# Issuing w_in earlier and putting pairs 6 to 12 and the weights on one software DMA queue, in a fused attention and MLP kernel

## The chip, the cores and the metric

The kernel runs on one core of one Trainium2 chip. The metric is the device time of one execution in microseconds (us). Executions of this kernel spread by one to two per cent. Two things in the traces differ from execution to execution: stretches of *half clock*, in which the trace's record of the clock granted to TensorE shows 0.5 instead of 1.0, and the rate of the DMA engines. So small differences are read from ratios with their 95% interval and from traces. "Ratio" below is always the mean time of one kernel's fast runs over that of the other kernel's fast runs of the same rounds, so it is not quite the ratio of the medians that are quoted. A difference under 2% is called "the same".

In the views PE is TensorE, PEld its weight loads, DVE VectorE, ACT ScalarE, POOL GpSimd and SP SyncE.

## The reference

```
q, k, v: float32 (8 batches, 12 heads, 448 rows, 64)
attn = softmax(q @ k.T / 8) @ v                        # per batch and head
x    = attn, heads side by side: (3584, 768)
h    = x @ w_in                                        # w_in (768, 2048) float32
out  = max(0.01 * h, h) @ w_out                        # w_out (2048, 768) float32; out (3584, 768)
```

## The kernel before

Work on attention is cut into 48 *pairs* (two heads of one batch; six pairs are a batch). For each pair, q, k and v come by DMA as float32 (three loads of 224 KB), GpSimd casts them to bf16, TensorE (for the first twelve pairs) transposes q and k, then computes scores and the product with v. When a batch is ready, the MLP over it is interleaved with the attention of the next batch. The first batch is done in twelve *halves* so that the first MLP can start after about 30 us.

Two kinds of DMA queue are in play. Loads of pairs are issued by SyncE on a hardware queue. The weights, which are cast on the way, are issued by GpSimd on a software queue; w_in in four column quarters, w_out in two row halves times two column halves. In each case at most eight transfers of an issuer are in flight: the trace shows eight semaphores for each, and a further issue waits until one has landed.

```python
    def load(u, queues=(nc.sync,) * 3):           # three DMAs: q, k, v of pair u
        ...                                       # buffers: five pairs in rotation
    def cast(u, by=(nc.gpsimd.tensor_copy,) * 3):
        ...

    for i in range(4):
        w_steps.append((w_in_sb[:, :, ts(i, DF // 4)], w_in_v[:, :, ts(i, DF // 4)]))
    for i in range(4):
        at = (slice(None), ts(i % 2, MD // 2), ts(i // 2, NW))
        w_steps.append((w_out_sb[at], w_out_v[at]))

    load(0, (nc.sync, nc.scalar, nc.sync))
    for i in range(1, 5):
        load(i)
    # ... memsets
    cast(0, (nc.vector.tensor_copy, nc.scalar.copy, nc.gpsimd.tensor_copy))
    cast(1)
    cast(2)
    # ... in the half stage, after half h:
    half_loads = {0: 5, 5: 6, 8: 7, 10: 8}
    half_casts = {1: 3, 3: 4, 5: 5, 8: 6, 10: 7}
    half_w = {5: 4, 8: 2, 10: 2}                  # how many weight pieces to issue
    half_turns = {1: 1, 2: 2, 4: 3, 5: 4, 7: 5, 11: 6}   # TensorE transposes of these pairs
    # ... later, pair by pair (u = 6, 7, ...):
    loads = {6: (9,), 7: (10, 11), 8: (12, 13)}   # then u + 5
    #   transposes(u + 1), cast(u + 3) (and cast(8) at u = 6)
    # second matmul of the first MLP: first column half of all chunks, then the second
        todo = [(c, w) for c in range(n // P) for w in range(2)]
        if i == 0:
            todo.sort(key=lambda cw: cw[1])
```

The softmax here doesn't subtract the row's maximum and nothing guards it: scores larger than these inputs give would overflow.

Of the kernel before, what the change touches and what calls it, by code (L numbers as in the profile page):

```python
# [9 lines left out]
F32 = mybir.dt.float32  # L10
# [6 lines left out]
def kernel(  # L17
# [9 lines left out]
    nc = tc.nc  # L27

    B, H, S, D = q.shape
    DM, DF = moe_w_in.shape  # L30
    P = 128
    HP = H // 2
# [3 lines left out]
    MD = DF // P  # L36
    NW = DM // 2
# [3 lines left out]
    cuts = [((b * S) // P) * P for b in range(B)] + [B * S]  # L41
# [15 lines left out]
    o_pool = ctx.enter_context(tc.tile_pool(name="o", bufs=3))  # L57
# [4 lines left out]
    ps_mm = ctx.enter_context(tc.tile_pool(name="ps_mm", bufs=2, space=PSUM))  # L62
# [23 lines left out]
    w_out_sb = w_pool.tile([P, MD, DM], BF16)  # L86
    w_in_v = moe_w_in.rearrange("(ko ki) n -> ki ko n", ki=P)
    w_out_v = moe_w_out.rearrange("(ko ki) n -> ki ko n", ki=P)
# [6 lines left out]
    def load(u, queues=(nc.sync,) * 3):  # L95
        if u >= NU:
            return
        b, hp = divmod(u, HP)
        raw[u] = []
        for a, name, eng in zip((q, k, v), ("fq", "fk", "fv"), queues):  # L100
            t = ld_pool.tile([SC, 2, NSC, D], F32, name=name)
            eng.dma_start(  # L102
                out=t.rearrange("p h so d -> p h (so d)"),
                in_=a[b, 2 * hp:2 * hp + 2].rearrange("h (p so) d -> p h (so d)", so=NSC),
            )
            raw[u].append(t)

    def cast(u, by=(nc.gpsimd.tensor_copy,) * 3):
        if u >= NU:
            return  # L110
        fq, fk, fv = raw.pop(u)
        qk_sb[u] = cast_pool.tile([SC, 2, NSC, 2, D], BF16, name="qkb")
        by[0](qk_sb[u][:, 0].rearrange("p so h d -> p h so d"), fq)  # L113
        by[1](qk_sb[u][:, 1].rearrange("p so h d -> p h so d"), fk)  # L114
        by[2](v_sb[u % NV][:, :, :, :D], fv)  # L115

    w_steps = []
    for i in range(4):
        w_steps.append((w_in_sb[:, :, ts(i, DF // 4)], w_in_v[:, :, ts(i, DF // 4)]))
    for i in range(4):  # L120
        at = (slice(None), ts(i % 2, MD // 2), ts(i // 2, NW))
        w_steps.append((w_out_sb[at], w_out_v[at]))

    def load_w(n=1):
        for _ in range(n):
            if w_steps:
                o, i = w_steps.pop(0)
                nc.gpsimd.dma_start(out=o, in_=i)  # L128
# [8 lines left out]
    def warm_up(n):  # L137
        for _ in range(n):
            ps = ps_mm.tile([P, 512], F32, name="mm")
            nc.tensor.matmul(ps, warm[:, :P], warm, start=True, stop=True)  # L140
# [10 lines left out]
        nc.gpsimd.memset(t[:, QL:], 0.0)  # L151
    cast(0, (nc.vector.tensor_copy, nc.scalar.copy, nc.gpsimd.tensor_copy))
    cast(1)
    cast(2)


    x_t = {}
# [76 lines left out]
    def half_scores(h, cp):  # L234
        u, ph = halves[h]
        ps = ps_s.tile([P, 2, 512], F32, name="sc")
        t = qkT[u % NQ]
        for i in range(2):
            c = 2 * cp + i
            for j in range(2):  # L240
                nc.tensor.matmul(  # L241
                    ps[:, j, ts(i, SH)],
                    t[j * D:(j + 1) * D, S + c * SC:S + c * SC + P],
                    t[j * D:(j + 1) * D, ts(ph, SH)],
                    start=True, stop=True,
                )
        e = e_sb[h % NE][:, :EH].rearrange("p (j c s) -> p j c s", j=2, c=NSC)
        nc.scalar.activation(  # L248
            e[:, :, 2 * cp:2 * cp + 2, :],
            ps[:SC, :, :S].rearrange("p j (c s) -> p j c s", c=2), AX.Exp, scale=scale,  # L250
        )
# [25 lines left out]
    def half_x_transposes(h):  # L277
        u, ph = halves[h]
        x = xh_t.pop(h)
        tr = ps_tr.tile([P, 2, S], BF16, name="tr")  # L280
        for qc in range(2):
            nc.tensor.transpose(tr[:, 0, ts(qc, SC)], x[:, qc], ident[:SC, :SC])
        nc.vector.tensor_copy(xT[:, u, ts(ph, SH)], tr[:, 0, :SH])
        if u == HP - 1:
            ready[0] = (ph + 1) * SH


    def store(o, t0):

        done = 0  # L290
        while done < P:
            b, j = divmod(t0 + done, S)
            so, p = divmod(j, SC)
            n = min(SC - p, P - done)
            dst = out[b * S:(b + 1) * S].rearrange("(p so) n -> so p n", so=NSC)
            nc.sync.dma_start(out=dst[so, p:p + n], in_=o[done:done + n, :])
            done += n

    def mlp(i):
        n = cuts[i + 1] - cuts[i]  # L300
        at = cuts[i] % NX
        h = h_pool.tile([P, MD, 4 * P], BF16, name="h")
        for lo, hi in ((0, SH), (SH, n)) if i == 0 else ((0, n),):
            for m in range(MD):
                ps = ps_mm.tile([P, 4 * P], F32, name="mm")
                assert i or hi <= ready[0]
                for kk in range(KD):
                    nc.tensor.matmul(  # L308
                        ps[:, :hi - lo], w_in_sb[:, kk, ts(m, P)], xT[:, kk, at + lo:at + hi],
                        start=(kk == 0), stop=(kk == KD - 1),  # L310
                    )
                    if kk == KD - 1:
                        nc.scalar.activation(  # L313
                            h[:, m, lo:hi], ps[:, :hi - lo], AX.Prelu, alpha=0.01
                        )
                    yield hi - lo

        todo = [(c, w) for c in range(n // P) for w in range(2)]
        if i == 0:
            todo.sort(key=lambda cw: cw[1])  # L320
        o = {}
        for c, w in todo:
            if c not in o:
                o[c] = o_pool.tile([P, DM], F32, name="o")
            ps = ps_mm.tile([P, 4 * P], F32, name="mm")
            for m in range(MD):
                nc.tensor.matmul(  # L327
                    ps[:, :NW], h[:, m, ts(c, P)], w_out_sb[:, m, ts(w, NW)],
                    start=(m == 0), stop=(m == MD - 1),
                )  # L330
                if m == MD - 1:
                    nc.vector.tensor_copy(o[c][:, ts(w, NW)], ps[:, :NW])  # L332
                    if w == 1:
                        store(o.pop(c), cuts[i] + c * P)
                yield NW


    loads = {6: (9,), 7: (10, 11), 8: (12, 13)}
    half_loads = {0: 5, 5: 6, 8: 7, 10: 8}
    half_casts = {1: 3, 3: 4, 5: 5, 8: 6, 10: 7}  # L340
    half_w = {5: 4, 8: 2, 10: 2}
    half_turns = {1: 1, 2: 2, 4: 3, 5: 4, 7: 5, 11: 6}

    def half_slots(h):


        def s0():
            half_scores(h, 0)

        def s1():  # L350
            if h == 0:
                warm_up(2)
            if h >= 2:
                half_x_transposes(h - 2)

        def s2():
            half_scores(h, 1)
            if h == 0:
                warm_up(2)

        def s3():
            if h in half_turns:
                transposes(half_turns[h])
            if h >= 1:
                half_pv(h - 1)
            if h in half_loads:
                load(half_loads[h])
            if h in half_casts:
                cast(half_casts[h])
            load_w(half_w.get(h, 0))  # L370

        return [s0, s1, s2, s3]

# [2 lines left out]
    def slots(u):  # L376

        on = u < NU

        def s0():  # L380
            if on:
                scores(u, 0)
                scores(u, 1)
                expo(u, 0)

        def s1():
            if on:
                expo(u, 1)
            if u - HP < 2:
                half_x_transposes(NH - 2 + u - HP)  # L390
            elif u <= NU + 1:
                x_transposes(u - 2)
            dma_transposes(u + 2)

        def s2():
            if u == HP:
                half_pv(NH - 1)
            elif u <= NU:
                pv(u - 1, 0)

        def s3():
            for i in loads.get(u, (u + 5,)):
                load(i)
            if u + 1 < NU:
                transposes(u + 1)

        def s4():
            if on:
                scores(u, 2)
                scores(u, 3)  # L410
                expo(u, 2)

        def s5():
            if on:
                expo(u, 3)
            if u == HP:
                cast(u + 2)
            cast(u + 3)

        def s6():  # L420
            if HP < u <= NU:
                pv(u - 1, 1)

        def s7():
            pass

        return [s0, s1, s2, s3, s4, s5, s6, s7]

    steps = [s for h in range(NH) for s in half_slots(h)]
# [9 lines left out]
    for i in range(B):  # L439
        work = steps[begin[i]:begin[i + 1]] if i + 1 < B else []  # L440
        n = cuts[i + 1] - cuts[i]
# [42 lines left out]
```

## Time and profile before

| | before |
|---|---|
| time, median of 3 (range) | 437.7 us (437.5 to 439.06) |
| profiled execution | 442.64 us, span 440.8 us |
| TensorE idle for w_in | 9.7 us in three waits |
| half clock in the trace's clock record | 32.8 to 39.6 us and 53.3 to 60.1 us |
| first w_in DMA: issued, first packet, landed | 22.2, 27.3, 35.6 us |
| last w_in quarter landed; last w_out piece landed | 54.3; 74.7 us |

From 60 us on TensorE is never short of work for long, so only the first 60 us can give time. The first view is of TensorE's waits over the whole kernel before: who waited, for whom, total us, number of times, longest.

```profile
PE mm L308 <- DMA w_in_sb<-in_moe_w_in_dram: 9.7, 3, 5.8
PE tr L282 <- DVE xh L269: 3.2, 9, 0.5
```

The timeline of TensorE before shows where: start, duration, the operation, and in brackets the idle time in front of it and what ended it.

```profile
35.63 1.12 PE L308 MATMUL mm<-xT,w_in_sb 128*128 128x224 bf16 x5 [5.77 <-DMA w_in_sb<-in_moe_w_in_dram]
...
48.04 2.03 PE L308 MATMUL mm<-xT,w_in_sb 128*128 128x224 bf16 x19 [0.89 <-DMA w_in_sb<-in_moe_w_in_dram]
...
54.32 1.11 PE L308 MATMUL mm<-xT,w_in_sb 128*128 128x224 bf16 x5 [3.08 <-DMA w_in_sb<-in_moe_w_in_dram]
```

GpSimd's timeline before has the four issues of w_in in one line, only after the cast of pair 5:

```profile
22.21 3.43 POOL L128 DMA_DIRECT2D w_in_sb<-in_moe_w_in_dram  x4
```

And the table by stretches before (from:to, length, busy us of PE, PEld, DVE, ACT and POOL with the number of instructions, granted TensorE clock, share of the DMA engines, GB/s written; the share can exceed 1, as the times of packets overlap):

```profile
30.00:35.00 5.00, 0.00 (x0) 0.00 (x0) 0.00 (x0) 0.88 (x1) 3.60 (x6) 0.78 1.18 246
35.00:40.00 5.00, 4.37 (x39) 3.27 (x40) 0.67 (x3) 1.27 (x3) 1.73 (x3) 0.54 1.18 245
...
50.00:55.00 5.00, 1.92 (x16) 1.28 (x16) 0.28 (x1) 2.33 (x4) 0.00 (x0) 0.83 1.19 248
55.00:60.00 5.00, 5.00 (x43) 3.52 (x42) 1.23 (x3) 1.45 (x3) 0.00 (x0) 0.50 1.22 248
```

A wait costs twice: the idle time itself, and the work behind it that runs at half clock (0.54 and 0.50). Meanwhile the DMA engines are full in every row. w_in is not late because the engines rest; it is late because other bytes went first: by 27 us the hardware queue alone had fetched more pairs than the six that the half stage needs.

### The profile page before, as it was taken

What the parts mean: (1) busy time and instruction counts of PE and PEld (TensorE: products, weight loads), DVE (VectorE), ACT (ScalarE), POOL (GpSimd) and SP (SyncE); (2) the same over time, 40 slices, a digit from 0 to 9 for tenths busy, and PEclk for the clock granted to TensorE, in tenths of its full rate; (3) what the DMA queues carried; (4) which work ended last, traced back from release to release, by engine and by line L of the source; (5) the groups of instructions that cost most, each with busy time, mean ns of one, the idle gap of its engine ahead of it and who ended that gap; (6) DMA issues with size and microseconds to landing.
All of it is one profiled execution on the core that took longest, in us unless ns stands there. A gap on an engine that the chain in (4) does not pass through costs nothing.

```text
span 440.8 us, 9314 instructions
## 1 busy us (share of the span) xinstructions
PE 419.2 (95%) x3875; PEld 235.6 (53%) x3875; DVE 102.0 (23%) x289; ACT 233.6 (53%) x338; POOL 92.2 (21%) x171
## 2 busy tenths in 40 slices
PE   8757699999999999999999999999999999999995
PEld 3535476654455555554455555554455555554563
DVE  2531122432122211232122211232122211220021
ACT  4763657656753377545753377545753477304300
POOL 4593112232211121313111131313111100000000
PEclk9997979999999999999999999999999999999999
DMA  9999999378655677587555687577555531130022
GB/s 200 237 241 245 246 231 201 42 218 211 132 110 139 171 186 173 138 167 186 117 107 143 165 200 168 133 162 192 115 107 144 152 87 26 48 81 13 0 73 71
DMA packets 98506, 63.67 MB, mean 144 GB/s; under 512 B 55456, under 2 KB 94880, under 8 KB 98464
## 3 DMA queue, kind: packets, MB, share of 16 engines
q1 hardware_dynamic: 90928, 56.56, 55.1%
q0 software_dynamic: 7296, 6.29, 8.8%
q8 instruction: 30, 0.49, 0.5%
q10 hardware_dynamic: 240, 0.23, 0.2%
q14 instruction: 12, 0.10, 0.1%
HBM read 45.61 MB, written 11.01 MB: 128 GB/s over the span
## 4 chain that ended last, share of the span: by engine, by line
PE 86%; DMA 11%; POOL 1%; issue 0%; ACT 0%; DVE 0%; SPq 0%; POOLq 0%
PE mm L327 34%; PE mm L308 33%; PE pv L204 10%; PE sc L186 9%; DMA w_in_sb<-in_moe_w_in_dram 7%; DMA fv<-in_v_dram 2%; DMA fq<-in_q_dram 2%; DMA fk<-in_k_dram 1%; PE tr L174 0%; POOL w_in_sb L128 0%; ACT e L195 0%; POOL v L115 0%; PE tr L225 0%; DVE o L332 0%; SPq L102 0%
## 5 line engine op out<-in xcount | busy, mean ns | idle before, releaser
L195 ACT ACTIVATE e<-sc 112x896 bf16<-112x896 f32 x168 | 148.1, 915 | 100.1 <-PE sc L186 99.6
L308 PE MATMUL mm<-xT,w_in_sb 128*128 128x512 bf16 (+3 forms) x864 | 167.4, 337 | 10.4 <-DMA w_in_sb<-in_moe_w_in_dram 9.7
L327 PE MATMUL mm<-w_out_sb,h 128*128 128x384 bf16 x896 | 161.2, 326 | 0.0
L308 PEld LDWEIGHTS <-w_in_sb 128*128 128x128 bf16 x864 | 76.5, 99 | 80.3 <-issue 18.1
L327 PEld LDWEIGHTS <-h 128*128 128x128 bf16 x896 | 81.3, 98 | 62.3 <-issue 14.8
L313 ACT ACTIVATE h<-mm 128x512 bf16<-128x512 f32 (+3 forms) x144 | 72.5, 504 | 71.5 <-PE mm L308 71.2
L115 POOL CAST v<-fv 112x512 bf16<-112x512 f32 x48 | 29.7, 618 | 236.3 <-PE pv L204 203.0
L211 DVE RECIPROCAL rec<-pv 112x4 f32<-112x4 f32 x84 | 15.3, 183 | 204.9 <-PE pv L204 204.7
L204 PEld LDWEIGHTS <-e 112*128 112x128 bf16 x1344 | 54.5, 98 | 12.2
L204 PE MATMUL pv<-v,e 112*128 112x65 bf16 x1344 | 57.2, 194 | 0.0
L332 DVE COPY o<-mm 128x384 f32<-128x384 f32 x56 | 31.2, 557 | 85.0 <-PE mm L327 84.7
L186 PE MATMUL sc<-qkT 64*128 64x448 bf16 x336 | 46.7, 357 | 0.0
L212 DVE TENSOR_TENSOR x<-pv,rec 112x256 bf16<-112x256 f32 x84 | 35.6, 424 | 2.9
L113 POOL CAST qkb<-fq 112x512 bf16<-112x512 f32 x47 | 29.0, 616 | 19.6 <-DMA fq<-in_q_dram 12.1
L114 POOL CAST qkb<-fk 112x512 bf16<-112x512 f32 x47 | 29.0, 616 | 4.5 <-DMA fk<-in_k_dram 4.0
L248 ACT ACTIVATE e<-sc 112x896 bf16<-112x896 f32 x24 | 21.5, 916 | 6.9 <-PE sc L241 6.6
L186 PEld LDWEIGHTS <-qkT 64*128 64x128 bf16 x336 | 9.6, 94 | 27.5 <-issue 23.6
L241 PE MATMUL sc<-qkT 64*128 64x224 bf16 x96 | 9.0, 266 | 1.6 <-DVE qkT L177 1.3
L177 DVE COPY qkT<-tr 128x896 bf16<-128x896 bf16 x12 | 7.5, 625 | 10.3 <-PE tr L174 10.2
L261 PE MATMUL pv<-v,e 112*128 112x65 bf16 x192 | 8.6, 198 | 0.0
L261 PEld LDWEIGHTS <-e 112*128 112x128 bf16 x192 | 7.6, 101 | 0.8 <-issue 0.6
L174 PE MATMUL tr<-ident,qkb 112*128 112x112 bf16 x96 | 7.4, 223 | 0.3
(28 smaller groups left out, 47.1 us busy)
## 6 DMA issues: line engine op xcount, KB each, us to landing
fq<-in_q_dram SPq DMA_DIRECT2D x48, 224.0 KB, 3.8
fv<-in_v_dram SPq DMA_DIRECT2D x48, 224.0 KB, 4.0
fk<-in_k_dram SPq DMA_DIRECT2D x47, 224.0 KB, 4.0
w_in_sb<-in_moe_w_in_dram POOLq DMA_DIRECT2D x4, 768.0 KB, 21.3
w_out_sb<-in_moe_w_out_dram POOLq DMA_DIRECT2D x4, 768.0 KB, 38.4
out_dram<-o SPq DMA_DIRECT2D x8, 336.0 KB, 3.0
out_dram<-o SPq DMA_DIRECT2D x8, 288.0 KB, 2.7
out_dram<-o SPq DMA_DIRECT2D x8, 240.0 KB, 3.1
```

Of the source, the lines that this page charges most:

```text
L113: by[0](qk_sb[u][:, 0].rearrange("p so h d -> p h so d"), fq)
L114: by[1](qk_sb[u][:, 1].rearrange("p so h d -> p h so d"), fk)
L115: by[2](v_sb[u % NV][:, :, :, :D], fv)
L186: nc.tensor.matmul(ps[:, j, :S], t[j * D:(j + 1) * D, S + c * SC:S + c * SC + P], t[j * D:(j + 1) * D, :S], start=True, stop=True,)
L195: nc.scalar.activation(e[:, :, c, :], sc_t.pop((u, c))[:SC, :, :S], AX.Exp, scale=scale)
L204: nc.tensor.matmul(ps[:, qc, :], e[:, at:at + P], vt[:, j, c, :], start=(c == 0), stop=(c == NSC - 1),)
L212: nc.vector.tensor_mul(x_t[u][:, :, j, :], ps[:SC, :, :D], rec.to_broadcast([SC, NSC, D]))
L248: nc.scalar.activation(e[:, :, 2 * cp:2 * cp + 2, :], ps[:SC, :, :S].rearrange("p j (c s) -> p j c s", c=2), AX.Exp, scale=scale,)
L308: nc.tensor.matmul(ps[:, :hi - lo], w_in_sb[:, kk, ts(m, P)], xT[:, kk, at + lo:at + hi], start=(kk == 0), stop=(kk == KD - 1),)
L313: nc.scalar.activation(h[:, m, lo:hi], ps[:, :hi - lo], AX.Prelu, alpha=0.01)
L327: nc.tensor.matmul(ps[:, :NW], h[:, m, ts(c, P)], w_out_sb[:, m, ts(w, NW)], start=(m == 0), stop=(m == MD - 1),)
L332: nc.vector.tensor_copy(o[c][:, ts(w, NW)], ps[:, :NW])
```

## The change

Intent: have w_in there when the first MLP starts, and give TensorE the rest in the order of use. Two quarters of w_in are issued between the casts of the first pairs. Pairs 6 to 12 leave the hardware queue and stand with the weights in the one software queue. w_out comes in four row quarters, and the second matmul of the first MLP takes its chunks in plain order. The casts of pairs 9 to 11 also move back by one pair in the program (`casts`).

```diff
-        at = (slice(None), ts(i % 2, MD // 2), ts(i // 2, NW))
-        w_steps.append((w_out_sb[at], w_out_v[at]))
+        w_steps.append((w_out_sb[:, ts(i, MD // 4), :], w_out_v[:, ts(i, MD // 4), :]))
     cast(1)
+    load_w()
     cast(2)
+    load_w()
-        if i == 0:
-            todo.sort(key=lambda cw: cw[1])
 ... (the loop over chunks c and column halves w in plain order)
-    loads = {6: (9,), 7: (10, 11), 8: (12, 13)}
-    half_loads = {0: 5, 5: 6, 8: 7, 10: 8}
-    half_w = {5: 4, 8: 2, 10: 2}
+    behind = {5: (6, "w", "w", 7), 8: ("w", "w", 8), 10: ("w", "w", 9)}
+    behind_pair = {6: (10,), 7: (11,), 8: (12,)}
+    casts = {6: (8,), 7: (9,), 8: (10,), 9: (11, 12)}
+    def issue(what):
+        for i in what:
+            if i == "w":
+                load_w()
+            else:
+                load(i, (nc.gpsimd,) * 3)
 ... (in slots:)
-            for i in loads.get(u, (u + 5,)):
-                load(i)
+            if u >= 8:
+                load(u + 5)
```

More of the change, by code (lines that the diff above doesn't have):

```diff
@@ L316, in mlp @@
                     yield hi - lo
-        todo = [(c, w) for c in range(n // P) for w in range(2)]
-        if i == 0:
-            todo.sort(key=lambda cw: cw[1])
-        o = {}
-        for c, w in todo:
-            if c not in o:
-                o[c] = o_pool.tile([P, DM], F32, name="o")
-            ps = ps_mm.tile([P, 4 * P], F32, name="mm")
-            for m in range(MD):
-                nc.tensor.matmul(
-                    ps[:, :NW], h[:, m, ts(c, P)], w_out_sb[:, m, ts(w, NW)],
-                    start=(m == 0), stop=(m == MD - 1),
-                )
-                if m == MD - 1:
-                    nc.vector.tensor_copy(o[c][:, ts(w, NW)], ps[:, :NW])
-                    if w == 1:
-                        store(o.pop(c), cuts[i] + c * P)
-                yield NW
-    loads = {6: (9,), 7: (10, 11), 8: (12, 13)}
-    half_loads = {0: 5, 5: 6, 8: 7, 10: 8}
-    half_casts = {1: 3, 3: 4, 5: 5, 8: 6, 10: 7}
-    half_w = {5: 4, 8: 2, 10: 2}
+        for c in range(n // P):
+            o = o_pool.tile([P, DM], F32, name="o")
+            for w in range(2):
+                ps = ps_mm.tile([P, 4 * P], F32, name="mm")
+                for m in range(MD):
+                    nc.tensor.matmul(
+                        ps[:, :NW], h[:, m, ts(c, P)], w_out_sb[:, m, ts(w, NW)],
+                        start=(m == 0), stop=(m == MD - 1),
+                    )
+                    if m == MD - 1:
+                        nc.vector.tensor_copy(o[:, ts(w, NW)], ps[:, :NW])
+                    yield NW
+            store(o, cuts[i] + c * P)
+    half_casts = {1: 3, 3: 4, 5: 5, 8: 6, 10: 7}
+    behind = {5: (6, "w", "w", 7), 8: ("w", "w", 8), 10: ("w", "w", 9)}
[7 more added lines that the diff above has]
+                load(i, (nc.gpsimd,) * 3)
     half_turns = {1: 1, 2: 2, 4: 3, 5: 4, 7: 5, 11: 6}
@@ L365, in s3 @@
                 half_pv(h - 1)
-            if h in half_loads:
-                load(half_loads[h])
+            if h == 0:
+                load(5)
             if h in half_casts:
                 cast(half_casts[h])
-            load_w(half_w.get(h, 0))
+            issue(behind.get(h, ()))
         return [s0, s1, s2, s3]
@@ L415, in s5 @@
                 expo(u, 3)
-            if u == HP:
-                cast(u + 2)
-            cast(u + 3)
+            for i in casts.get(u, (u + 3,)):
+                cast(i)
+            issue(behind_pair.get(u, ()))
         def s6():
```

## The prediction

> **What bounds the kernel now.** From 60 us on TensorE is busy in every window (the windows view shows 10.00 of 10 us to 400 us), so only the first 60 us can give time. There the waits view puts 9.7 us of TensorE idleness on the landing of w_in: 5.8 us before the first MLP matmul at 35.6, 0.9 before 48.0, 3.1 before 54.3. After the long gaps the granted clock is 0.54 (35 to 40 us) and 0.50 (55 to 60 us), where about 4 and 5 us of work run at half rate: another 4.5 us, an estimate. Sum: about 14 us. The Trainium skill (TensorE: Matmul & The Clock Gate, Part 1) tells of a free-running window of about 3.4 us after which an idle array is halved; the trace agrees.
>
> The reason is DMA order. Until 27 us the hardware queue alone runs, at 237 to 242 GB/s (0.97 us for each 224 KB load), and has fetched some ten pairs although the half stage needs six. The first w_in DMA is issued at 22.2 us, its first packet moves at 27.3; then both queues share and a quarter of w_in lands only every 6.3 us. The last w_in lands at 54.3, w_out not until 74.
>
> **What the change does.** Two quarters of w_in are issued at about 9.5 and 13 us. With the same 5 us of delay they flow from 14.6 us beside pairs 4 and 5 (84 packets per engine, 0.131 us per pair of packets of the two queues): pair 5 lands at about 25.6 instead of 21.5. I expect its transposes to wait 1 to 2 us, and the MLP to start near 31 to 32 us with two quarters present. The w_in waits go.
>
> But the rest is in one queue behind the cast of pair 5: about 27 us, then a bubble of about 2 us in the DMA engines. From there, sequentially: a pair 2.9 us (at the rate of a queue alone), a weight quarter 3.8 us (w_out alone read about 410 GB/s of f32 at 62 to 66 us). Pair 6 at 31.5, w_in complete at 39, pair 7 at 42, w_out's first half at 50, pair 8 at 53, w_out complete at 61, pair 9 at 63 to 65, later if pair 13 on the hardware queue mixes in. TensorE would want the transposes of pairs 7, 8 and 9 at about 39, 47 and 54: so the waits for w_in become waits for q and k of pairs 7, 8, 9 (2 to 4 us each, half clock behind some). Pair 9's transposes ran at 65.3 before; I expect 61 to 66. The software issues cost GpSimd 0.75 us each, 16 us in all, beside 21% busy: off the path. The row quarters of w_out make packets of 1536 instead of 768 bytes[...]: nearly nothing. The new order of the second matmul's chunks: nothing, as w_out lands before 74.
>
> **Prediction.** Of the 14 us most comes back as waits for pairs: 436.5 us, 430.5 to 442.5 eight times in ten. Faster by over 2%: 0.07, same: 0.86, slower: 0.07.
>
> **What would show it.** Right: no wait for w_in; TensorE first MLP matmul near 32 us; waits of transposes for casts of pairs 7 to 9, GpSimd waiting on landing q, k of those; a half clock between 40 and 65. Wrong: TensorE without a gap after 32 us (then some 10 us faster), or w_in waits that remain.
>
> **What would make it wrong.** The software queue alone moving 1 KB packets faster or slower than 0.07 us each; a start delay of 5 us at each software issue; GpSimd held at an issue (eight may be in flight) while a cast is due; gaps too short for the clock to fall.

## The result, and the profile after

| | before | changed |
|---|---|---|
| median (range), 4 runs each | 438.02 us (437.5 to 439.06) | 440.73 us (440.39 to 441.48) |
| ratio, 95% interval | | 1.0061 (1.0037 to 1.0085) |
| span of the profiled execution | 440.8 us | 438.6 us |
| TensorE idle for w_in | 9.7 us | 0 |
| TensorE idle for casts of pairs 7, 8, 9 | 0 | 8.1 us |
| half clock | 6.8 + 6.8 us | 3.4 + 3.4 us |

The timed runs say the same within 2%, a little slower. The two profiled executions seem to say the opposite (438.6 against 440.8), because the one of before fell in a slow execution with long stretches of half clock.

TensorE's waits after:

```profile
PE tr L175 <- POOL qkb L113: 6.8, 3, 3.2
PE tr L283 <- DVE xh L270: 3.2, 9, 0.5
...
PE tr L175 <- POOL qkb L114: 1.2, 3, 0.6
```

The waits for w_in have gone, and new ones of nearly the same sum have come: the transposes (tr) of q and k wait for GpSimd's casts (qkb). TensorE's timeline after has them one by one. The first line is the first MLP matmul, at 29.8 instead of 35.6 us and without a gap:

```profile
29.76 0.65 PE L309 MATMUL mm<-xT,w_in_sb 128*128 128x224 bf16 x5
...
41.37 0.37 PE L175 MATMUL tr<-ident,qkb 112*128 112x112 bf16 x4 [2.92 <-POOL qkb L113]
...
52.64 0.37 PE L175 MATMUL tr<-ident,qkb 112*128 112x112 bf16 x4 [3.20 <-POOL qkb L113]
53.57 0.56 PE L175 MATMUL tr<-ident,qkb 112*128 112x112 bf16 x4 [0.57 <-POOL qkb L114]
...
62.53 0.37 PE L175 MATMUL tr<-ident,qkb 112*128 112x112 bf16 x4 [0.71 <-POOL qkb L113]
63.39 0.37 PE L175 MATMUL tr<-ident,qkb 112*128 112x112 bf16 x4 [0.49 <-POOL qkb L114]
```

These are pairs 7, 8 and 9. GpSimd's timeline after shows what held the casts, here for pair 8: the cast of k waited for the DMA. (The line above it is an issue that waited for one of the eight transfers in flight.)

```profile
51.20 0.66 POOL L102 DMA_DIRECT2D fv<-in_v_dram  x1 [4.81 <-DMA w_out_sb<-in_moe_w_out_dram]
51.97 0.61 POOL L113 CAST qkb<-fq 112x512 bf16<-112x512 f32 x1
52.90 0.61 POOL L114 CAST qkb<-fk 112x512 bf16<-112x512 f32 x1 [0.32 <-DMA fk<-in_k_dram]
```

A wait put down to GpSimd is thus a wait for a landing. q of pair 8 landed at 51.91 us and its cast began at 51.97; q of pair 7 at 40.39 and 40.69. In this kernel the hold at issues cost at most 0.3 us.

The stretches after, beside those shown of before:

```profile
40.00:45.00 5.00, 3.46 (x27) 2.42 (x28) 0.62 (x1) 2.19 (x4) 4.58 (x7) 0.81 1.15 212
45.00:50.00 5.00, 4.44 (x48) 3.32 (x46) 0.88 (x3) 3.05 (x7) 0.68 (x1) 0.85 1.11 268
50.00:55.00 5.00, 1.80 (x14) 1.15 (x16) 0.62 (x1) 0.36 (x1) 3.12 (x6) 0.84 1.14 229
55.00:60.00 5.00, 5.00 (x59) 3.49 (x56) 0.61 (x2) 3.64 (x7) 1.29 (x2) 0.82 1.15 238
```

Again full DMA engines, an idle TensorE, and half clock in or behind the two long gaps.

### The profile page after: what moved, and what is told of

Same layout as the page of the kernel before. It is cut to its first block, busy times and chain, and to the rows that moved or that the text cites. A ratio compares the mean times of both kernels' runs of the same rounds, so it can differ in the third digit from the quotient of the medians.

```text
span 438.6 us, 9307 instructions
## 1 busy us (share of the span) xinstructions
PE 418.5 (95%) x3875; PEld 234.6 (53%) x3875; DVE 102.0 (23%) x289; ACT 233.3 (53%) x338; POOL 105.2 (24%) x192
## 4 chain that ended last, share of the span: by engine, by line
PE 87%; DMA 7%; DVE 2%; POOL 2%; issue 1%; ACT 1%; POOLq 0%
PE mm L323 34%; PE mm L309 31%; PE pv L205 9%; PE sc L187 9%; DMA fk<-in_k_dram 4%; DMA w_out_sb<-in_moe_w_out_dram 3%; PE tr L175 1%; PE mm L139 1%; DVE qkT L178 1%; DVE xh L270 1%; ACT e L249 0%; PE tr L283 0%; POOL fq L102 0%; PE sc L242 0%; POOL fk L102 0%
## 5 line engine op out<-in xcount | busy, mean ns | idle before, releaser
L323 PEld LDWEIGHTS <-h 128*128 128x128 bf16 x896 | 81.3, 98 | 62.3 <-issue 14.8
L212 DVE RECIPROCAL rec<-pv 112x4 f32<-112x4 f32 x84 | 15.3, 183 | 201.1 <-PE pv L205 200.9
L205 PEld LDWEIGHTS <-e 112*128 112x128 bf16 x1344 | 54.0, 98 | 12.2
L205 PE MATMUL pv<-v,e 112*128 112x65 bf16 x1344 | 56.8, 194 | 0.0
L213 DVE TENSOR_TENSOR x<-pv,rec 112x256 bf16<-112x256 f32 x84 | 35.6, 424 | 2.9
L175 PEld LDWEIGHTS <-qkb 112*128 112x128 bf16 x96 | 5.8, 100 | 11.4 <-POOL qkb L113 7.5
```

The costliest lines, as they stand in the source:

```text
L205: nc.tensor.matmul(ps[:, qc, :], e[:, at:at + P], vt[:, j, c, :], start=(c == 0), stop=(c == NSC - 1),)
L213: nc.vector.tensor_mul(x_t[u][:, :, j, :], ps[:SC, :, :D], rec.to_broadcast([SC, NSC, D]))
L323: nc.tensor.matmul(ps[:, :NW], h[:, m, ts(c, P)], w_out_sb[:, m, ts(w, NW)], start=(m == 0), stop=(m == MD - 1),)
```

## The experiments

Theory A: the loss is in what stands in front of what; with weights and pairs 6 to 12 in one queue, the pairs come after weights that nobody needs yet. Rivals: B, total bytes are the limit and an early w_in displaces the pairs in any queue; C, the row quarters and the new chunk order cost time; D, the software queue or GpSimd's issues are slow by themselves.

### The kernel before once more: b_again

> The kernel before, unchanged, for a profile in the fast state. Its first profile was of state slow (span 440.8 us against a median time of 438.0) with two half-clock stretches of 6.8 us. I expect a span near 436 us, the same three waits for w_in (together 9 to 10 us), and a shorter time at half clock.

Measured: 441.67 us for the one run (before in that job: median 439.78, 438.45 to 441.79), span 439.9. Waits for w_in 8.5 us, half clock from 31.0 to 41.2 and 54.9 to 58.3 us. The hope for a shorter half clock failed (13.7 us in all, as in the first profile): the clock differs from execution to execution of one kernel. The state was unknown; it agrees with the first profile in the mechanism.

### Only the early w_in: early

```diff
 kernel before
     cast(1)
+    load_w()
     cast(2)
+    load_w()
-    half_w = {5: 4, 8: 2, 10: 2}
+    half_w = {5: 2, 8: 2, 10: 2}
```

> The kernel before with one part of the change: the first two w_in quarters issued between the casts of pairs 1 and 2, pairs still on the hardware queue. Theory A (the loss is that weights and pairs 6 to 12 stand in one queue, one after the other, so that the pairs come late): no wait for w_in and none for the pairs, about 429 us, 2% faster than before. Rival B (w_in early only displaces the pairs, whatever queue they are in; total bytes are the limit): 436 to 441 us with waits of transposes for casts.

Measured: 429.27 us (429.24 to 430.13) against 439.78, ratio 0.9759 (0.9725 to 0.9793): faster. B falls. TensorE waits neither for w_in nor for a pair nor for w_out, and the clock never drops between 30 and 60 us:

```profile
40.00:45.00 5.00, 4.38 (x57) 3.66 (x55) 0.59 (x3) 4.33 (x9) 1.85 (x3) 1.00 1.21 249
45.00:50.00 5.00, 4.87 (x67) 3.68 (x66) 1.52 (x4) 3.71 (x9) 1.85 (x3) 1.00 1.21 250
50.00:55.00 5.00, 4.62 (x75) 3.80 (x73) 1.62 (x4) 3.97 (x9) 1.85 (x3) 1.00 1.22 249
```

### The change with pairs 6 to 12 on the hardware queue: hw_pairs

```diff
 changed kernel
-                load(i, (nc.gpsimd,) * 3)
+                load(i)
```

> The changed kernel with pairs 6 to 12 given back to the hardware queue, all else kept. Theory A: the three waits before the transposes of pairs 7, 8 and 9 (8.1 us in all) go, 429 to 431 us. Rival B: they remain, or come back as waits for w_in or w_out, 437 us or more. Rival C (the row quarters of w_out and the new order of the second matmul cost time): stays above 436 us with the waits gone.

Measured: 430.99 us (429.19 to 432.5), ratio to before 0.9791 (0.9739 to 0.9842; by the interval unclear at 2%). The three waits for casts are gone, by this one line. In their place stand only 0.5 us for w_in at 44.0 and 1.0 us for w_out at 65.7:

```profile
44.04 0.65 PE L309 MATMUL mm<-xT,w_in_sb 128*128 128x224 bf16 x5 [0.51 <-DMA w_in_sb<-in_moe_w_in_dram]
...
65.67 0.32 PE L323 MATMUL mm<-w_out_sb,h 128*128 128x384 bf16 x1 [0.98 <-DMA w_out_sb<-in_moe_w_out_dram]
```

So taking the pairs off the hardware queue was the change's loss. The line does two things, though: it gives the pairs a queue of their own, and it lets SyncE issue them earlier (q of pair 8 at 22.4 instead of 32.4 us). The next runs, in which GpSimd goes on issuing the pairs, tell more. A faster DMA is no rival: in this execution a load landed every 0.97 us before 15 us, in that of the changed kernel every 0.90. The 1.0 us is a first hint at rival C.

### One queue, but pairs 8 to 10 before w_out: pairs_first

```diff
 changed kernel
-    behind = {5: (6, "w", "w", 7), 8: ("w", "w", 8), 10: ("w", "w", 9)}
-    behind_pair = {6: (10,), 7: (11,), 8: (12,)}
+    behind = {5: (6, "w", "w", 7), 8: (8, 9), 10: ("w", "w", 10)}
+    behind_pair = {6: ("w", "w"), 7: (11,), 8: (12,)}
```

> The changed kernel with the one software queue kept, but pairs 8, 9 and 10 ahead of w_out's quarters. Theory A: the wait at pair 7 stays (2.9 us, it stands behind w_in in any case), those at pairs 8 and 9 (3.8 and 1.2 us) and the half clock behind them go: 433 to 435 us. Rival D (software descriptors or the issues on GpSimd are slow by themselves): the waits stay, 438 us or more.

Measured: 435.16 us, ratio 0.9888 (0.985 to 0.9927). The waits at pairs 8 and 9 are gone, the one at pair 7 stands at 4.4 us (2.9 expected). As pairs 8 and 9 are still issued by GpSimd on the software queue, rival D does not explain their waits in the changed kernel; what stood in front of them does: q of pair 8 was issued at 31.8 us (32.4 in the changed kernel) and landed at 43.3 (51.9). Here the hold at issues does show: q of pair 7 landed at 41.1 us, but GpSimd stood at the issue of v of pair 9 and cast only at 42.3:

```profile
41.65 0.66 POOL L102 DMA_DIRECT2D fv<-in_v_dram  x1 [0.96 <-DMA fq<-in_q_dram]
42.31 0.62 POOL L113 CAST qkb<-fq 112x512 bf16<-112x512 f32 x1
```

### One queue in order of need: deadline

```diff
 changed kernel, these lines in place of its own
+    behind = {5: (6, 7, "w", "w"), 8: (8, 9), 10: ("w", "w", 10)}
+    behind_pair = {6: ("w", "w"), 7: (11,), 8: (12,)}
```

> The changed kernel with everything still in the one software queue, but in the order in which TensorE came to need it in the fast variants: pairs 6 and 7, w_in's second half, pairs 8 and 9, half of w_out, pair 10, the other half, pairs 11 and 12. Theory A' (the order in the one queue is what loses, not the kind of queue): no wait of transposes over 1 us, 429 to 432 us, as fast as with pairs on the hardware queue. Rival D (the software queue moves pairs too slowly, or GpSimd is held at issues): waits of 2 us and more remain, 434 us or more.

Measured: 435.09 us (432.89 to 436.31, 6 runs), ratio 0.9896 (0.984 to 0.9952). Half a miss: better than the change, not as good as the hardware queue. In the profiled execution, the fastest of the six, TensorE waits for pair 8, for pair 11, and for the last quarter of w_out:

```profile
46.41 0.37 PE L175 MATMUL tr<-ident,qkb 112*128 112x112 bf16 x4 [1.23 <-POOL qkb L113]
...
67.19 0.32 PE L323 MATMUL mm<-w_out_sb,h 128*128 128x384 bf16 x1 [1.25 <-DMA w_out_sb<-in_moe_w_out_dram]
...
69.75 0.37 PE L175 MATMUL tr<-ident,qkb 112*128 112x112 bf16 x4 [0.35 <-POOL qkb L114]
```

So the strong form of A, that the order in one queue is all, fell. For what is left D is not excluded: the time lies where D was expected (434 us or more), though the longest wait is 1.25 us and not 2. The cast of pair 8 was held at an issue (k landed at 43.4 us, GpSimd stood at issues until 45.7).

### Pair 13 kept back: late13

Pair 13 was still loaded by the hardware queue. Its load stands before that of pair 12 in the program and starts as soon as the cast of q of pair 7 has ended (41.3 us), so it ran beside w_out and pair 8.

```diff
 changed kernel
-    behind_pair = {6: (10,), 7: (11,), 8: (12,)}
+    behind_pair = {6: (10,), 7: (11,), 8: (12, 13)}
-            if u >= 8:
+            if u >= 9:
                 load(u + 5)
```

> The changed kernel with pair 13 moved from the hardware queue, where it was issued at 41.3 us and ran beside w_out and pairs 8 and 9, to the end of the software queue. If pair 13 delays the software queue there: k of pair 8 lands about 2 us earlier than 52.9 us and k of pair 9 about 2 us earlier than 62.7, ratio to the changed kernel 0.995. If the queue is bound by its own order alone: the same within 0.3%.

Measured: 439.25 us, ratio to before 0.9984 (0.9934 to 1.0033); the changed kernel on the same chip (after_again) 441.2. Ratio of the two means, 439.17 / 441.21 = 0.9954; by the scatter of four runs each it is uncertain by about 0.005 (an estimate). k of pair 8 landed at 50.65 instead of 52.71, k of pair 9 at 60.51 instead of 62.50. The landings moved as expected. That the time followed by 0.5% is not clear of noise.

### Only the row quarters and the chunk order: rows_only

The kernel before, with the first and the third group of the change's diff (w_out by row quarters, chunks in plain order) and nothing else.

> The kernel before with only w_out by row quarters and the second matmul's chunks in plain order. My prediction gave both nothing: ratio to before within 0.5% of 1, w_out packets of 1536 instead of 768 bytes, the waits for w_in unchanged. Rival C (they cost time in the changed kernel): 1% or more over before; it would show as a wait for w_out at the start of the second matmul near 74 us.

Measured: 440.29 us, ratio 0.9993 (0.9935 to 1.0052). No wait for w_out. In the kernel before C is false: no cost or gain of these parts shows, to within 0.6%. The waits for w_in stay, 8.2 us:

```profile
33.86 1.11 PE L307 MATMUL mm<-xT,w_in_sb 128*128 128x224 bf16 x5 [3.94 <-DMA w_in_sb<-in_moe_w_in_dram]
...
46.36 2.02 PE L307 MATMUL mm<-xT,w_in_sb 128*128 128x224 bf16 x19 [1.17 <-DMA w_in_sb<-in_moe_w_in_dram]
...
52.66 0.65 PE L307 MATMUL mm<-xT,w_in_sb 128*128 128x224 bf16 x5 [3.10 <-DMA w_in_sb<-in_moe_w_in_dram]
```

### The changed kernel once more: after_again

> The changed kernel, unchanged, for the comparison on the same chip: 440.7 us, ratio to before 1.006, waits of 2.9, 3.8 and 1.2 us before the transposes of pairs 7, 8 and 9.

Measured: 441.2 us (439.88 to 442.55), ratio 1.003 (0.9975 to 1.0085). Waits of 2.6, 4.9 and 1.2 us at pairs 7, 8 and 9; the half clock came only once, 53.2 to 56.6 us.

### The hold at issues removed: no_hold

```diff
 deadline
-    behind = {5: (6, 7, "w", "w"), 8: (8, 9), 10: ("w", "w", 10)}
-    behind_pair = {6: ("w", "w"), 7: (11,), 8: (12,)}
+    behind = {5: (6, 7, "w", "w"), 8: (8, 9), 10: ("w", "w")}
+    behind_pair = {6: (10, "w", "w"), 7: (11,), 8: (12,)}
```

> The one-queue kernel in order of need, with the three loads of pair 10 issued after the cast of pair 8 instead of before it. In the run of that order GpSimd stood at these issues until 45.7 us (eight transfers in flight), though k of pair 8 had landed at 43.4, and TensorE waited 1.2 us for the cast. If the hold is the cause: the cast of pair 8 starts within 0.5 us of landing, the wait at pair 8's transposes is under 0.3 us, and the time is 1 to 2 us lower (433 to 434 us). If the landing itself was late: no change.

Measured: 437.66 us, ratio 0.9944 (0.9896 to 0.9992): a miss. The cast of q of pair 8 did start right after landing (44.44 to 44.50 us), and the wait at pair 8 fell to 0.85 us. But k of pair 8 itself landed at 45.7 instead of 43.4, and w_out only at 70.3, and TensorE now waited there:

```profile
66.54 0.48 PE L323 MATMUL mm<-w_out_sb,h 128*128 128x384 bf16 x2 [1.57 <-DMA w_out_sb<-in_moe_w_out_dram]
...
70.38 0.48 PE L323 MATMUL mm<-w_out_sb,h 128*128 128x384 bf16 x1 [2.44 <-DMA w_out_sb<-in_moe_w_out_dram]
```

This job ran on another chip than that of deadline; the loads before 15 us landed every 0.96 us in its profile and every 0.89 in deadline's, so the two times are not compared to a per cent. What stands is that the hold was not the main loss.

### A tiny software transfer at the start: warm_sw

```diff
 early
+    tiny = const_pool.tile([P, 16], F32)
+    nc.gpsimd.dma_start(out=tiny, in_=moe_w_in[:P, :16])
     load(0, (nc.sync, nc.scalar, nc.sync))
```

In the profiles of all runs the first w_in packet moves 4.4 to 6.3 us after its issue. The run asks whether that is a cost of the first software transfer.

> The kernel with w_in issued early and pairs on the hardware queue, plus one tiny software transfer (16 columns) at the very start. [...]If that is a cost of the first software transfer: now 1 to 2 us after the issue at 9 us, so first w_in packet near 11 us. If it comes from the loads that stand ahead in the hardware queue: unchanged, near 14.5 us. The time stays 429 to 431 us either way.

Measured (one look): 429.44 us. The first w_in DMA, issued at 9.3 us, again moved its first packet only at 14.95 us. The delay is not a cost of first use. That it comes from the hardware loads ahead of it agrees with this, but is not shown; the tiny transfer itself, issued at 1.3 us, did not land until 5.1 to 6.2.

### One queue in order of need, w_out as before: deadline_cols and no_hold_cols

Both are the kernels deadline and no_hold with w_out cut into row and column halves and the first column half of all chunks used first, as in the kernel before. In early the last piece of w_out landed at 71.4 us without a wait; with row quarters all four are wanted within the first chunk.

> The one-queue kernel in order of need, with w_out cut and used as in the kernel before: two row halves by two column halves, the first column half of all chunks first. In the run with row quarters TensorE waited 1.25 us for the last quarter of w_out (landed 67.2), while in the fast variant with column halves the last piece landed at 71.4 without any wait, as it is not wanted before the last third of the second matmul. If the cut is what the one-queue order still lost: no wait for w_out, ratio to before 0.980 or less (it was 0.990). If not: 0.987 to 0.993, with the waits elsewhere.

> The same with pair 10 issued after the cast of pair 8. In the run with row quarters this variant waited 4.0 us for w_out (last quarter landed 70.3) and fell to half clock at 69 us. With column halves: no wait for w_out and no half clock there, ratio to before 0.982 or less (it was 0.994); the cast of pair 8 within 0.5 us of its landing.

Measured: deadline_cols 433.87 us, ratio 0.9878 (0.9818 to 0.9938); no_hold_cols 436.49 us, ratio 0.992 (0.9879 to 0.9961). The wait for w_out is gone in both, so in these faster kernels the row quarters did cost; but the time hardly followed. The wait moved to pair 11, which stands behind w_out's second half in the queue:

```profile
69.75 0.37 PE L176 MATMUL tr<-ident,qkb 112*128 112x112 bf16 x4 [1.63 <-POOL qkb L113]
```

That is the line of deadline_cols; in no_hold_cols the same wait is 2.98 us. The expected ratios (0.980 and 0.982 or less) were missed; for deadline_cols what was said for the other case, 0.987 to 0.993 with the waits elsewhere, came. no_hold_cols, expected without half clock there, had it from 69.7 to 73.1 us.

### Adding it up

The gaps before 110 us that end with a DMA or a cast, and half of the busy time at half clock (an estimate from the clock record), account for nearly all differences between the profiled executions, although these ran on several chips and at different DMA rates:

| kernel | span, us | gaps | half of the busy time at half clock | span less both |
|---|---|---|---|---|
| before | 440.8 | 9.7 | 4.9 | 426.2 |
| b_again | 439.9 | 8.5 | 4.5 | 426.9 |
| rows_only | 438.1 | 8.2 | 3.1 | 426.7 |
| changed | 438.6 | 8.1 | 3.3 | 427.2 |
| after_again | 438.4 | 8.7 | 1.6 | 428.1 |
| late13 | 437.4 | 5.8 | 4.6 | 426.9 |
| no_hold | 436.4 | 5.5 | 2.9 | 428.0 |
| pairs_first | 434.4 | 4.4 | 3.0 | 427.1 |
| no_hold_cols | 432.7 | 3.9 | 1.5 | 427.2 |
| deadline_cols | 431.9 | 3.9 | 0 | 427.9 |
| deadline | 431.1 | 3.0 | 0 | 428.1 |
| hw_pairs | 429.2 | 1.5 | 0 | 427.7 |
| early | 427.5 | 0 | 0 | 427.5 |

The spans differ by 13.4 us, what is left of them by 1.9.

Is it that two queues move more? Float32 read by the moments named, summed from the trace's packets (weight packets counted double, as they are halved on the way; the one load of ScalarE's queue, 0.23 MB in every run, left out), in MB:

| | 30 us | 40 us | 50 us | 60 us |
|---|---|---|---|---|
| before (b_again) | 6.7 | 10.4 | 14.1 | 17.7 |
| changed | 8.2 | 11.9 | 15.7 | 19.5 |
| deadline | 8.4 | 12.0 | 15.3 | 19.0 |
| hw_pairs | 8.2 | 11.9 | 15.7 | 19.5 |
| early | 8.5 | 12.2 | 15.8 | 19.4 |

The changed kernel read as much as early and hw_pairs. It read other things. In us, the landings of k (from the trace), beside the moment at which TensorE transposed the pair in early, where nothing held it:

| | wanted | before (b_again) | changed | hw_pairs | early | deadline |
|---|---|---|---|---|---|---|
| k of pair 7 | 38.2 | 26.3 | 41.1 | 33.8 | 32.7 | 30.3 |
| k of pair 8 | 44.9 | 29.0 | 52.9 | 39.6 | 38.4 | 43.4 |
| k of pair 9 | 51.9 | 34.3 | 62.7 | 46.2 | 43.9 | 46.9 |
| last w_in quarter | | 54.3 | 39.5 | 44.0 | 42.4 | 41.0 |
| last w_out piece | | 75.3 | 61.0 | 65.6 | 71.4 | 67.2 |

The changed kernel had w_in and w_out complete earliest and the pairs latest. With two queues the engines alternate between them: from 36 to 42 us of early, 771 packets of the hardware queue and 769 of the software queue were moved. So pairs and weights advance side by side, and both were in time. In the same 6 us of the changed kernel the hardware queue moved none.

## Why the prediction was right or wrong, point by point

The range (430.5 to 442.5) held; 440.7 was measured against 436.5 as the most likely value, so against before the change was expected to win 1.5 us and lost 2.7.

- *"The w_in waits go", and "the waits for w_in become waits for q and k of pairs 7, 8, 9 (2 to 4 us each, half clock behind some)".* Right, but for pair 9, whose wait is shorter than said: 2.9, 3.8 and 1.2 us, half clock at 43.1 to 46.5 and 53.4 to 56.8. hw_pairs takes these waits away by one line, and pairs_first those of pairs 8 and 9 by the order in the queue alone.
- *The arrivals from the sum of sequential transfers* (pair 7 at 42, pair 8 at 53, pair 9 at 63 to 65). Right: v of these pairs landed at 41.7, 53.7 and 63.5. That pair 13 would mix in was right too, 2 us by late13.
- *"Pair 5 lands at about 25.6", transposes waiting 1 to 2 us, MLP start near 31 to 32.* Wrong in size: pair 5 landed at 22.9, nothing waited, the MLP started at 29.8. By 14.8 us q of pair 4 had landed, a load more than I had reckoned, and in this execution loads landed every 0.90 us, not every 0.97 as in the profile that I had read. The "some ten pairs" fetched by 27 us were nearly nine.
- *"A bubble of about 2 us".* Did not come: pair 6 was issued at 23.6 us, while the second w_in quarter was still moving (landed 26.9).
- *"Nearly nothing" for the row quarters.* Right for the kernel before (0.9993) and for the change, wrong as a general statement: where the rest is fast, they bring a wait of 1.0 to 4.0 us.
- *GpSimd's issues "off the path".* Right for the change; in pairs_first and deadline an issue held a cast by about 1 us or more.
- *The loss of before, "about 14 us".* This is the term that put 436.5 too low. It was read from a slow execution with 13.7 us of half clock, the most that was seen (b_again has as much, and loses 13.0 us in a run of 441.67). In rows_only, whose executions take as long as those of before, gaps and half clock come to 8.2 + 3.1 = 11.3 us, and the change has 8.1 + 3.3 = 11.4. The two cancel. That the changed kernel is 0.6% slower (1.0037 to 1.0085; 0.9975 to 1.0085 in after_again) is not explained by this sum.

The skill's statement that I leaned on (TensorE: Matmul & The Clock Gate, Part 1) holds here in that the half clock lasts multiples of 3.4 us (3.4, 6.8, 10.2) and differs from run to run. It does not hold in that a whole window must be idle: the 3.4 us before the drop at 53.3 us of before had 1.4 us of matmul in them.

What stays open: why the one-queue kernels in order of need still end 1% behind early. Their residual waits moved from place to place (pair 8, w_out, pair 11) as each was mended; pair 13 on the hardware queue, the holds of issues and the fixed order may all take part, and no run here separates them. Their size can be read: the profiled deadline has gaps of 3.0 us and no half clock before 110 us, while its five other executions show a mean granted clock of 0.994 to 0.996 instead of 0.999. That is 1.3 to 2.2 us more (an estimate: the difference times 433 us), so short gaps and the half clock that some of them bring make up most of the 5.8 us between 435.09 and early's 429.27.

## What to carry to other kernels

Issue the weights early, but leave them in another queue than the stream that TensorE consumes all the time: with two queues both advanced here, and neither stood in front of the other. If one queue must hold both, order it by the moment of need of each piece, not by group, and look for streams beside it that were forgotten (pair 13). Best here was the smallest edit: early, 429.3 us, 2.4% under the kernel before.

## What the Trainium skill lacked or had wrong

- DMA: Bandwidth & Descriptors, "Issuing engines are not separate DMA queues": it says that issuing from several engines only saves issue time. As to bandwidth the runs agree (15.7 and 15.8 MB read by 50 us). What the section lacks is what the choice of queue does to the order of landing, though the page's part on arbitration says that the engines take the queues in turn: k of pair 8 landed at 52.9 us in one queue, at 39.6 in two, and the times are 440.73 and 430.99 us.
- The same page, "Latency and other measured facts", gives about 1 us to the first byte of a software transfer. Beside a busy hardware queue the first w_in packet moved 4.4 to 6.3 us after its issue, also with an earlier software transfer (5.7 us in warm_sw); that tiny transfer, issued at 1.3 us, moved its first packet after 2.8 us.
- TensorE: Matmul & The Clock Gate, "Why this matters for your kernels", advises no idle gap over about 3 us. In late13 half clock began in or after gaps of 1.96 and 2.06 us, while one of 2.40 us in after_again stayed without: shorter gaps can be enough. The 3.4 us before the first of these drops (39.9 us) had 1.7 us of matmul in them.
- No page compares the packets of the two kinds of queue for one load: the software queue's copies of 224 KB went as packets of 4096 and 2048 bytes, the hardware queue's of the same loads as 1024. The rate was about the same: where pair 7 followed pair 6 directly on the software queue (deadline, no_hold and their column forms), 0.77 to 0.96 us a load, and on the hardware queue of the same runs before 15 us 0.87 to 0.96.
